# Two branches of cached attention for one token: one weight buffer split in two, K and V rings of four, the last V in pieces

## Chip, cores, metric

The kernel runs on one core of a Trainium2 chip. The metric is the device time of one execution in microseconds (us). Before the change it is 1589.96 us, the median of four runs (1573.62, 1588.67, 1591.26 and 1592.13). The run with a profile is the one of 1573.62 us; its trace spans 1571.9 us.

## What is computed

Two branches, A and B, have the same shape: one new token of width 512, 32 heads of width 128, and a cache of 8192 keys and values for each head, all in bf16. For each branch:

```python
q = (x @ wq) as 32 heads of 128          # x: 1 x 512, wq: 512 x 4096
scores = (q . k_cache) * 128 ** -0.5     # 8192 scores for each head
p = softmax(scores)
o = p . v_cache                          # 128 for each head
out = concat(o over heads) @ wo          # wo: 4096 x 512
# result: A's out and B's out side by side, 1 x 1024
```

The cache of one head is 2 MB of K and 2 MB of V, each read once. The kernel counts the heads of both branches through, n = 0 to 63; B begins with n = 32.

## The kernel before

K and V of a head lie in SBUF as 128 partitions by 64 keys by 128 values (`kb`, `vb`), in rings of three. Both wq and, later, both wo share one buffer `wb`. SyncE issues all loads; a load into a used place waits until its last reader is done.

```python
kb = SB("kb", [128, NK, JT, 128], BF)          # NK = 3, JT = 64
vb = SB("vb", [128, NV, JT, 128], BF)          # NV = 3
wb = SB("wb", [128, NBR, WSZ], BF)             # wq of both, then wo of both

# SyncE: x of both branches, then
for b in range(NBR):
    sp.dma_start(wb[:, b, ...], wqv[b]).then_inc(s_wq, 16)
def dma_k(n):
    if n >= NK:                                # the multiplies of head n-3 are done
        W(sp, s_tf, NE * (n - NK + 1)); W(sp, s_sttd, NDS * (n - NK + 1))
    sp.dma_start(kb[:, n % NK], ...)
def dma_v(n):
    if n >= NV:                                # P.V of head n-3 is done
        W(sp, s_pvd, n - NV + 1)
    sp.dma_start(vb[:, n % NV], ...)
def dma_wo(n):
    W(sp, s_qp, 1)                             # wq is no longer read
    if n >= 4: W(sp, s_pjd, n - 3)
    sp.dma_start(wb[:, b, h * DO:(h + 1) * DO], ...)
dma_k(0)
for n in range(N):
    if n + 1 < N: dma_k(n + 1)
    dma_v(n); dma_wo(n)
```

TensorE waits for both wq and projects q for all 64 heads, four matmuls each (L215), before anything else. Then all engines run one list of steps t, eight for each head. In slots 0, 2 and 4 of a head TensorE transposes eight blocks of K (L245), ScalarE copies them (`kt`, L349), and TensorE multiplies them by q (L259). In slots 1, 3, 5, 6 and 7 VectorE multiplies eight blocks each by a copy of q on all partitions (`qrep`) and sums along each row (L418). ScalarE copies TensorE's scores beside VectorE's (`ssb`, L356). The softmax needs the largest score and the sum over all partitions, which GpSimd makes:

```python
for n in range(N):                             # GpSimd
    W(pl, s_rmx, n + 1)
    pl.partition_all_reduce(gmx[n], mx[n], 128, ROP.max)            # L200
    pl.tensor_scalar(nb[n], gmx[n], -scale, None, AluOpType.mult)   # L202
    W(pl, s_expd, n + 1)
    pl.partition_all_reduce(gs[n], rs[n], 128, ROP.add)             # L204

# ScalarE, step 10 after the head's first
psb = exp(scale * ssb + nb), with the row sums in rs                # L332

# VectorE, in this order in its program
mx[n] = max of ssb (step 9)                                         # L387
rinv[n] = 1 / gs[n] (step 13, that is ahead of slot 5 of head n+1)  # L392
oT[n] = sum of P.V times rinv (step 20)                             # L398
```

P times V runs on TensorE in four blocks (L278) from step 12 on, ScalarE copies the result (`dsb`, L342), four small matmuls gather it (L298), and one matmul adds the head's part of the output projection (L311) into `misc`. After head 31 and head 63 VectorE casts `misc` to the output (`osb`, L405).

Of the kernel before, what the change touches and what calls it, by code (L numbers as in the profile page):

```python
# [7 lines left out]
def bass_concat_heads__mha_block_cached__gqa_block_cached__decode_kernel(  # L8
# [5 lines left out]
    NK, NV, LPV, NPE = 3, 3, 12, 3  # L14
# [16 lines left out]
    assert DH == 128 and D % 128 == 0 and SK % 2048 == 0  # L31
# [5 lines left out]
    assert DO <= 512 and N <= 64 and JT <= 64 and NG % 2 == 0  # L37
    NPS = NPE
    assert 1 <= NPS <= NG // 2

    def is_pe_slot(g):
        return g % 2 == 0 and g // 2 < NPS

    pe_slots = [g for g in range(NG) if is_pe_slot(g)]
    dv_slots = [g for g in range(NG) if not is_pe_slot(g)]
    NPT = 8 * len(pe_slots)
    colmap = {}
    for i, g in enumerate(pe_slots):
        for r in range(8):
            colmap[8 * g + r] = 8 * i + r  # L50
    for i, g in enumerate(dv_slots):
        for r in range(8):
            colmap[8 * g + r] = NPT + 8 * i + r
# [7 lines left out]
    WSZ = max(NCH * H * 128, H * DO)  # L61
# [3 lines left out]
    with ExitStack() as es:  # L65
# [12 lines left out]
        wb = SB("wb", [128, NBR, WSZ], BF)  # L78
# [26 lines left out]
        s_x = SEM("s_x"); s_wq = SEM("s_wq")  # L105
        s_wo0 = SEM("s_wo0"); s_wo1 = SEM("s_wo1"); s_wo2 = SEM("s_wo2"); s_wo3 = SEM("s_wo3")
        s_kl0 = SEM("s_kl0"); s_kl1 = SEM("s_kl1"); s_kl2 = SEM("s_kl2"); s_kl3 = SEM("s_kl3")
        s_vl0 = SEM("s_vl0"); s_vl1 = SEM("s_vl1"); s_vl2 = SEM("s_vl2"); s_vl3 = SEM("s_vl3")
        s_id0 = SEM("s_id0"); s_idr = SEM("s_idr"); s_slr = SEM("s_slr"); s_dz = SEM("s_dz")
        s_qp = SEM("s_qp"); s_qt = SEM("s_qt")  # L110
# [9 lines left out]
        assert NK <= 4 and NV <= 4  # L120
        s_kl = [s_kl0, s_kl1, s_kl2, s_kl3][:NK]
        s_vl = [s_vl0, s_vl1, s_vl2, s_vl3][:NV]
        s_wo = [s_wo0, s_wo1, s_wo2, s_wo3]
# [11 lines left out]
        LAST_PE_QK = max(pe_slots) + 2  # L135
        ST_RMAX = NG + 1
        ST_EXP = NG + 2
        ST_PV = max(LPV, NG + 4)
# [7 lines left out]
        NE = len(pe_slots)  # L146
        NDS = len(dv_slots)

        @block.sync
        def _(sp):  # L150
            with nc.allow_non_contiguous_dma(reason="tiny x transpose load"):
                for b in range(NBR):
                    sp.dma_start(xT[:, b, :], xv[b]).then_inc(s_x, 16)  # L153
            for b in range(NBR):
                sp.dma_start(
                    wb[:, b, 0:NCH * H * 128].rearrange("p (c m) -> p c m", c=NCH), wqv[b]
                ).then_inc(s_wq, 16)

            def dma_k(n):
                b, h = br_of(n)  # L160
                if n >= NK:
                    W(sp, s_tf, NE * (n - NK + 1))
                    W(sp, s_sttd, NDS * (n - NK + 1))
                sp.dma_start(kb[:, n % NK], kvw[b][:, h]).then_inc(s_kl[n % NK], 16)

            def dma_v(n):
                b, h = br_of(n)
                if n >= NV:
                    W(sp, s_pvd, n - NV + 1)
                sp.dma_start(vb[:, n % NV], vvw[b][:, h]).then_inc(s_vl[n % NV], 16)  # L170

            def dma_wo(n):
                b, h = br_of(n)
                W(sp, s_qp, 1)
                if n >= 4:
                    W(sp, s_pjd, n - 3)
                sp.dma_start(wb[:, b, h * DO:(h + 1) * DO], wov[b][:, h, :]).then_inc(s_wo[n % 4], 16)

            dma_k(0)
            for n in range(N):  # L180
                if n + 1 < N:
                    dma_k(n + 1)
                dma_v(n)
                dma_wo(n)
            for b in range(NBR):
                W(sp, s_accd, b + 1)
                sp.dma_start(out[0, 0:1, b * DO:(b + 1) * DO], osb[0:1, b, :]).then_inc(s_outd, 16)
            sp.wait_ge(s_outd, 16 * NBR)

        @block.gpsimd  # L190
        def _(pl):
            pl.memset(ones[:, :], 1.0).then_inc(s_id0, 1)
            pl.wait_ge(s_id0, 1)
            pl.affine_select(
                ident[:, :], ones[:, :], [[1, 128]], AluOpType.is_equal, 0.0,
                base=0, channel_multiplier=-1,
            ).then_inc(s_idr, 1)
            for n in range(N):
                W(pl, s_rmx, n + 1)
                pl.partition_all_reduce(gmx[:, n:n + 1], mx[:, n:n + 1], 128, ROP.max).then_inc(s_g1, 1)  # L200
                W(pl, s_g1, n + 1)
                pl.tensor_scalar(nb[:, n:n + 1], gmx[:, n:n + 1], -scale, None, AluOpType.mult).then_inc(s_nbr, 1)  # L202
                W(pl, s_expd, n + 1)
                pl.partition_all_reduce(gs[:, n:n + 1], rs[:, n:n + 1], 128, ROP.add).then_inc(s_gsr, 1)  # L204

        @block.tensor
        def _(pe):
            W(pe, s_x, 16 * NBR)
            W(pe, s_wq, 16 * NBR)
            last = None  # L210
            for n in range(N):
                b, h = br_of(n)
                wqb = wb[:, b, 0:NCH * H * 128].rearrange("p (c m) -> p c m", c=NCH)
                for c in range(NCH):
                    last = pe.matmul(  # L215
                        misc[:, n:n + 1], wqb[:, c, h * 128:(h + 1) * 128], xT[:, b, c:c + 1],
                        start=(c == 0), stop=(c == NCH - 1),
                    )
            last.then_inc(s_qp, 1)
            W(pe, s_idr, 1)  # L220

# [10 lines left out]
            for t in range(-16, TMAX):  # L232
                n, g = t // NG, t % NG
                if (t - ST_QREP) % NG == 0 and 0 <= (t - ST_QREP) // NG < N:
                    qrep_mm((t - ST_QREP) // NG)
                if 0 <= n < N and is_pe_slot(g):
                    e = g // 2
                    E = NE * n + e
# [10 lines left out]
                if 0 <= n2 < N and is_pe_slot(g2):  # L249
                    e = g2 // 2  # L250
                    E = NE * n2 + e
                    if e == 0:
                        if n2 == 0:
                            W(pe, s_qt, 1)
                        W(pe, s_qre, n2 + 1)
                    W(pe, s_ev, E + 1)
                    for i in range(8):
                        j = g2 * 8 + i
                        ins = pe.matmul(  # L259
                            sbk[n2 % 2][:, colmap[j]:colmap[j] + 1], kt[:, E % 2, i * 128:(i + 1) * 128],  # L260
# [4 lines left out]
                if tp >= 0 and tp // NG < N and (tp % NG) % 2 == 0 and (tp % NG) // 2 < JT // 16:  # L265
                    n3 = tp // NG
                    bt = (tp % NG) // 2
                    if bt == 0:
# [3 lines left out]
                        W(pe, s_vl[n3 % NV], 16 * (n3 // NV + 1))  # L272
                        if n3 >= 2:
                            W(pe, s_devd, n3 - 1)
                    for c in range(4):
                        i = 4 * bt + c
                        c0 = colmap[4 * i]
# [26 lines left out]
                if tj >= 0 and tj % NG == 0 and tj // NG < N:  # L304
# [3 lines left out]
                    W(pe, s_wo[n5 % 4], 16 * (n5 // 4 + 1))  # L308
                    if h == 0 and b > 0:
                        W(pe, s_accd, b)  # L310
                    pe.matmul(  # L311
                        misc[0:1, 0:DO], oT[:, n5:n5 + 1], wb[:, b, h * DO:(h + 1) * DO],
# [4 lines left out]
        def _(act):  # L317
            for t in range(-16, TMAX):
                n, g = t // NG, t % NG
                if (t - ST_QREP) % NG == 0 and 0 <= (t - ST_QREP) // NG < N:  # L320
                    m = (t - ST_QREP) // NG
                    W(act, s_qrm, m + 1)
                    if m >= 2:
                        W(act, s_sttd, NDS * (m - 1))
# [18 lines left out]
                if 0 <= n < N and is_pe_slot(g):  # L343
                    e = g // 2
                    E = NE * n + e
# [6 lines left out]
                tc = t - (LAST_PE_QK + 1)  # L352
                if tc >= 0 and tc % NG == 0 and tc // NG < N:
                    n8 = tc // NG
                    W(act, s_qkd, NE * (n8 + 1))
                    act.activation(ssb[:, n8 % 2, 0:NPT], sbk[n8 % 2][:, 0:NPT], AF.Copy).then_inc(s_scp, 1)  # L356

        @block.vector
        def _(dve):
# [8 lines left out]
            dve.tensor_copy(qT[:, :], misc[:, 0:N]).then_inc(s_qt, 1)  # L368

            def diag_op(m):  # L370
                W(dve, s_qt, 1)
# [6 lines left out]
            for t in range(-16, TMAX):  # L378
# [4 lines left out]
                if tr >= 0 and tr % NG == 0 and tr // NG < N:  # L383
                    n1 = tr // NG
                    W(dve, s_sttd, NDS * (n1 + 1))
# [20 lines left out]
                if 0 <= n < N and not is_pe_slot(g):  # L406
                    first = (g == dv_slots[0])
                    Sd = NDS * n + dv_slots.index(g)
                    if first:
                        W(dve, s_kl[n % NK], 16 * (n // NK + 1))  # L410
                        W(dve, s_qre, n + 1)
                        if n >= 2:
                            W(dve, s_expd, n - 1)
                    if Sd >= 2:
                        W(dve, s_sttd, Sd - 1)
                    for i in range(8):
                        j = g * 8 + i
                        ins = dve.scalar_tensor_tensor(  # L418
                            junk[:, (Sd % 2) * 8 + i, :], kb[:, n % NK, j, :], 1.0, qrep[:, n % 2, :],
                            AluOpType.mult, AluOpType.mult,  # L420
                            accum_out=ssb[:, n % 2, colmap[j]:colmap[j] + 1],
                        )
                    ins.then_inc(s_sttd, 1)
# [28 lines left out]
```

## Time and profile before

| what | busy us, or value |
|---|---|
| span of the trace | 1571.9 |
| VectorE (DVE) | 598.0 |
| TensorE (PE), and its weight loads (PEld) | 409.4, 244.7 |
| ScalarE (ACT) | 186.0 |
| GpSimd (POOL) | 67.4 |
| read from HBM | 285.21 MB, 181 GB/s over the span |
| granted TensorE clock | 0.578 of full speed on average |
| one multiply of VectorE (L418), x2560 | 287 ns |
| one PARTITION_ALL_REDUCE (L200, L204), x64 each | 379 and 402 ns as recorded |
| K and V, 2048 KB: issue to landing | 7.9 and 12.6 |

Busy times add up each engine's instructions. No engine is busy for more than 38% of the span, so these sums alone don't tell what sets the time. The profile has three further views that do: the list of waits (who stood idle, and which instruction released it), the chain that ended last (followed back from the last instruction, step by step), and the timeline of one engine. "issue" in them is time in which an engine waited for nothing that the profile shows. POOLq is GpSimd's instruction sequencer. GpSimd's recorded spans are rough.

### The profile page before, as it was taken

The page shows a single profiled execution, that of the slowest core. Times are in us where ns is not written, and L with a number is a line of the kernel's source. Part 1 is how long each engine was busy: PE and PEld are TensorE (multiplying, and loading weights), DVE is VectorE, ACT ScalarE, POOL GpSimd, SP SyncE. Part 2 cuts the span into 40 slices and gives each one's busy share as a digit, 9 for nine tenths or more (in the row PEclk, how much of TensorE's full clock was granted, in tenths as well). Part 3 has the DMA queues.
Part 4 walks back from the last instruction along what each step waited for, and adds up shares of the span by engine and source line. Part 5 has one row for each costly group of instructions (what it writes and reads, how often), then busy time and mean ns, then how long its engine had stood idle before and what let it go on. Part 6 is the DMA issues. An engine that isn't in the chain of part 4 may idle for free.

```text
span 1571.9 us, 17244 instructions
## 1 busy us (share of the span) xinstructions
PE 409.4 (26%) x4736; PEld 244.7 (16%) x4736; DVE 598.0 (38%) x5382; ACT 186.0 (12%) x513; POOL 67.4 (4%) x198
## 2 busy tenths in 40 slices
PE   2132221231322313313213223133132231321331
PEld 2111111111111101101111111011111110111110
DVE  1433433424434334244244343342442433424433
ACT  0011011010110101101101101011011010110110
POOL 0000000000000000000000000000000000000000
PEclk9855555555555555555555555555555555555555
DMA  9735435345354453453543544534535435355330
GB/s 381 303 136 221 181 150 221 149 182 212 124 217 171 161 221 141 191 215 134 202 191 141 221 166 165 221 139 193 202 136 215 175 157 221 127 204 207 133 159 0
DMA packets 29860, 286.33 MB, mean 182 GB/s; under 512 B 4162, under 2 KB 12356, under 8 KB 12356
## 3 DMA queue, kind: packets, MB, share of 16 engines
q1 hardware_dynamic: 29764, 285.23, 46.0%
q8 instruction: 38, 0.62, 0.2%
q14 instruction: 58, 0.48, 0.1%
HBM read 285.21 MB, written 0.00 MB: 181 GB/s over the span
## 4 chain that ended last, share of the span: by engine, by line
issue 69%; DVE 22%; POOL 4%; DMA 1%; ACT 1%; POOLq 1%; PE 1%; ACTq 0%; SPq 0%; DVEq 0%
DVE junk L418 21%; POOL gs L204 2%; POOL gmx L200 2%; DMA wb<-in_B_wq_dram 1%; POOL nb L202 1%; DVE mx L387 1%; ACT psb L332 1%; DVE rinv L392 1%; PE misc L215 0%; POOLq L65 0%; POOLq L202 0%; ACTq L130 0%; DVE osb L405 0%; SPq L153 0%; PE misc L311 0%
## 5 line engine op out<-in xcount | busy, mean ns | idle before, releaser
L418 DVE SCALAR_TENSOR_TENSOR junk<-kb,qrep 128x128 bf16<-128x128 bf16 x2560 | 557.7, 287 | 1.1 <-ACT qrep L325 0.8
L259 PE MATMUL sb<-qT,kt 128*128 128x1 bf16 x1536 | 73.7, 169 | 1091.5 <-ACT kt L349 1091.5
L398 DVE TENSOR_SCALAR oT<-sb,rinv 128x1 bf16<-128x1 f32 x64 | 14.1, 221 | 659.5 <-PE sb L298 659.4
L259 PEld LDWEIGHTS sb<-qT,kt 128*128 128x128 bf16 x1536 | 67.0, 109 | 1104.5 <-ACT kt L349 1104.2
L418 DVE DVE_READ_ACCUMULATOR junk<-kb,qrep 128x1 f32 x2560 | 210.9, 82 | 0.1
L245 PE MATMUL tb<-ident,kb 128*128 128x128 bf16 x1536 | 181.0, 292 | 0.0
L332 ACT ACTIVATE psb<-ssb,nb 128x64 bf16<-128x64 f32 x64 | 22.4, 350 | 1183.2 <-POOL nb L202 1183.2
L278 PE MATMUL db<-vb,psb 128*4 128x512 bf16 x1024 | 148.1, 568 | 15.8 <-ACT psb L332 15.8
L245 PEld LDWEIGHTS tb<-ident,kb 128*128 128x128 bf16 x1536 | 136.3, 132 | 101.7 <-issue 101.7
L349 ACT ACTIVATE kt<-tb 128x512 f32<-128x512 f32 x192 | 113.3, 590 | 108.1 <-PE tb L245 108.1
L392 DVE RECIPROCAL rinv<-gs 128x1 f32<-128x1 f32 x64 | 10.5, 164 | 276.0 <-POOL gs L204 276.0
L202 POOL TENSOR_SCALAR nb<-gmx 128x1 f32<-128x1 f32 x64 | 16.7, 261 | 712.3 <-issue 712.3
L204 POOL PARTITION_ALL_REDUCE gs<-rs x64 | 25.8, 402 | 389.3 <-issue 389.3
L311 PE MATMUL misc<-wb,oT 128*1 128x512 bf16 x64 | 40.3, 630 | 3.0 <-DVE oT L398 3.0
L200 POOL PARTITION_ALL_REDUCE gmx<-mx x64 | 24.3, 379 | 390.0 <-DVE mx L387 390.0
L342 ACT ACTIVATE dsb<-db 128x512 bf16<-128x512 f32 x64 | 37.5, 586 | 2.2 <-PE db L278 2.2
L278 PEld LDWEIGHTS db<-vb,psb 128*4 128x4 bf16 x1024 | 23.3, 81 | 32.5 <-ACT psb L332 16.7
L325 ACT ACTIVATE qrep<-sb 128x128 bf16<-128x128 f32 x64 | 17.8, 278 | 84.7 <-PE sb L228 84.7
L228 PE MATMUL sb<-diag,ones 128*128 128x128 bf16 x64 | 16.9, 264 | 22.7 <-issue 22.0
L298 PE MATMUL sb<-sel,dsb 128*128 128x1 bf16 x256 | 17.1, 170 | 0.7 <-ACT dsb L342 0.7
L298 PEld LDWEIGHTS sb<-sel,dsb 128*128 128x128 bf16 x256 | 11.8, 107 | 29.2 <-ACT dsb L342 28.8
L374 DVE TENSOR_SCALAR diag<-ident,qT 128x128 bf16<-128x128 bf16 x64 | 16.0, 251 | 0.0
(19 smaller groups left out, 69.1 us busy)
## 6 DMA issues: line engine op xcount, KB each, us to landing
kb<-in_A_k_cache_dram SPq DMA_DIRECT2D x32, 2048.0 KB, 7.9
vb<-in_A_v_cache_dram SPq DMA_DIRECT2D x32, 2048.0 KB, 12.6
kb<-in_B_k_cache_dram SPq DMA_DIRECT2D x32, 2048.0 KB, 7.7
vb<-in_B_v_cache_dram SPq DMA_DIRECT2D x32, 2048.0 KB, 12.5
wb<-in_A_wq_dram SPq DMA_DIRECT2D x1, 4096.0 KB, 13.1
wb<-in_B_wq_dram SPq DMA_DIRECT2D x1, 4096.0 KB, 22.5
wb<-in_A_wo_dram SPq DMA_DIRECT2D x32, 128.0 KB, 12.3
wb<-in_B_wo_dram SPq DMA_DIRECT2D x32, 128.0 KB, 12.3
```

Of the source, the lines that this page charges most:

```text
L200: pl.partition_all_reduce(gmx[:, n:n + 1], mx[:, n:n + 1], 128, ROP.max).then_inc(s_g1, 1)
L202: pl.tensor_scalar(nb[:, n:n + 1], gmx[:, n:n + 1], -scale, None, AluOpType.mult).then_inc(s_nbr, 1)
L204: pl.partition_all_reduce(gs[:, n:n + 1], rs[:, n:n + 1], 128, ROP.add).then_inc(s_gsr, 1)
L245: ins = pe.transpose(tb[E % 2][:, i * 128:(i + 1) * 128], kb[:, n % NK, j, :], ident[:, :])
L259: ins = pe.matmul(sbk[n2 % 2][:, colmap[j]:colmap[j] + 1], kt[:, E % 2, i * 128:(i + 1) * 128], qT[:, n2:n2 + 1], start=True, stop=True,)
L278: ins = pe.matmul(dbk[n3 % 2][32 * c:32 * c + 4, 0:512], psb[:, n3 % 2, c0:c0 + 4], vb[:, n3 % NV, 4 * i:4 * i + 4, :].rearrange("p a d -> ...
L298: ins = pe.matmul(sbk[(n4 + 1) % 2][:, OC:OC + 1], dsb[:, n4 % 2, m * 128:(m + 1) * 128], sel[:, m:m + 1], start=(m == 0), stop=(m == 3),)
L311: pe.matmul(misc[0:1, 0:DO], oT[:, n5:n5 + 1], wb[:, b, h * DO:(h + 1) * DO], start=(h == 0), stop=(h == H - 1),).then_inc(s_pjd, 1)
L332: act.activation(psb[:, n6 % 2, :], ssb[:, n6 % 2, :], AF.Exp, bias=nb[:, n6:n6 + 1], scale=scale, accum_out=rs[:, n6:n6 + 1],).then_inc(s ...
L342: act.activation(dsb[:, n7 % 2, :], dbk[n7 % 2][:, :], AF.Copy).then_inc(s_devd, 1)
L349: act.activation(kt[:, E % 2, :].bitcast(F32), tb[E % 2][:, :].bitcast(F32), AF.Copy,).then_inc(s_ev, 1)
L418: ins = dve.scalar_tensor_tensor(junk[:, (Sd % 2) * 8 + i, :], kb[:, n % NK, j, :], 1.0, qrep[:, n % 2, :], AluOpType.mult, AluOpType.mult ...
```

## The change

Three buffers are laid out anew, with no change to the arithmetic of a head.

- `wb` becomes `wqs`, which holds one branch's wq, and `wos`, a ring of eight for single heads' parts of wo. A's wq is loaded first, B's into the same place once A's has been read. TensorE projects A's q at the start, and B's in heads 8 to 15, four heads at a time. A PSUM bank of their own, `qpb`, takes the results. The aim is that the first head need not wait for B's weights.
- The rings of K and V have four places instead of three, so that loads may run further ahead.
- V of the last head is loaded in four pieces with a semaphore each, so that P times V may begin with the first of them.

The rest is renaming: the map "PDPDPDDD" states which engine takes which slot of a head.

```diff
-    NK, NV, LPV, NPE = 3, 3, 12, 3
+    NK, NV, NWO, QB0, VCH, MAP = 4, 4, 8, 8, 4, "PDPDPDDD"
...
-        wb = SB("wb", [128, NBR, WSZ], BF)
+        wqs = SB("wqs", [128, NCH, H * 128], BF)
+        wos = SB("wos", [128, NWO, DO], BF)
...
+        qpb = PS("qpb", [128, 512], F32)
...
-        LAST_PE_QK = max(pe_slots) + 2
-        ST_PV = max(LPV, NG + 4)
+        ST_PV = NG + 4
...
-            for b in range(NBR):
-                sp.dma_start(
-                    wb[:, b, 0:NCH * H * 128].rearrange("p (c m) -> p c m", c=NCH), wqv[b]
-                ).then_inc(s_wq, 16)
+            sp.dma_start(wqs[:, :, :], wqv[0]).then_inc(s_wq, 16)
...
-                sp.dma_start(vb[:, n % NV], vvw[b][:, h]).then_inc(s_vl[n % NV], 16)
+                if n == N - 1 and VCH > 1:
+                    jc = JT // VCH
+                    for c in range(VCH):
+                        sp.dma_start(
+                            vb[:, n % NV, c * jc:(c + 1) * jc, :], vvw[b][:, h, c * jc:(c + 1) * jc, :]
+                        ).then_inc(s_vlc[c], 16)
+                else:
+                    sp.dma_start(vb[:, n % NV], vvw[b][:, h]).then_inc(s_vl[n % NV], 16)
...
-                W(sp, s_qp, 1)
-                if n >= 4:
-                    W(sp, s_pjd, n - 3)
-                sp.dma_start(wb[:, b, h * DO:(h + 1) * DO], wov[b][:, h, :]).then_inc(s_wo[n % 4], 16)
+                if n >= NWO:
+                    W(sp, s_pjd, n - NWO + 1)
+                sp.dma_start(wos[:, n % NWO, :], wov[b][:, h, :]).then_inc(s_wo[n % NWO], 16)
+
+            def dma_wq_b():
+                W(sp, s_qp, 1)
+                sp.dma_start(wqs[:, :, :], wqv[1]).then_inc(s_wqb, 16)
...
+            # order of issue: k0, then k(n+1), v(n), wo(n); B's wq behind wo(2)
...
-            W(pe, s_wq, 16 * NBR)
+            W(pe, s_wq, 16)
             last = None
-            for n in range(N):
+            for n in range(H):
+                last = qproj(n)
             last.then_inc(s_qp, 1)
...
+            QPB = 4
+            qb_sched = {}
+            for i in range(0, H, QPB):
+                qb_sched[min(QB0 + i // QPB, H - 2) * NG + 1] = list(range(H + i, min(H + i + QPB, N)))
...
+                if t in qb_sched:
+                    if qb_left[0] == len(qb_sched):
+                        W(pe, s_wqb, 16)
+                    for nn in qb_sched[t]:
+                        ins = qproj(nn)
...
-            dve.tensor_copy(qT[:, :], misc[:, 0:N]).then_inc(s_qt, 1)
+            dve.tensor_copy(qT[:, 0:H], qpb[:, 0:H]).then_inc(s_qt, 1)
...
+                if m >= H and not qt2_done[0]:
+                    W(dve, s_qp2, 1)
+                    dve.tensor_copy(qT[:, H:N], qpb[:, H:N]).then_inc(s_qt2, 1)
```

(The comment on the order of issue stands for a loop that builds the list.)

## The prediction

> **What bounds the kernel now.** I read the list of waits first, to see whether any engine ever waits for a K or V load. Columns: engine and line that waited, what released it, total us, times, longest us.
>
> ```profile
> ACT psb L332 <- POOL nb L202: 1183.2, 64, 21.9
> POOL nb L202 <- issue: 712.3, 64, 12.6
> POOL gmx L200 <- DVE mx L387: 390.0, 64, 34.2
> POOL gs L204 <- issue: 389.3, 64, 8.4
> DVE rinv L392 <- POOL gs L204: 276.0, 64, 16.2
> PE misc L215 <- DMA wb<-in_B_wq_dram: 25.0, 1, 25.0
> DVE junk L418 <- ACT qrep L325: 0.8, 1, 0.8
> ```
>
> The only wait for a load is PE's for B's wq, once, 25.0 us. The multiplies (L418) never wait for K. The long waits lead to GpSimd, and GpSimd's own two are "issue": nothing recorded ended them.
>
> Next, the chain that ended last, for one head in the middle (start us, length us, what):
>
> ```profile
> 731.92 5.61 issue
> 737.53 0.41 POOL gs L204
> 737.95 0.02 issue
> 737.97 0.17 DVE rinv L392
> 738.13 3.86 DVE junk L418 x37
> ...
> 743.25 0.23 DVE mx L387
> 743.48 0.09 issue
> 743.57 0.38 POOL gmx L200
> 743.95 0.06 POOLq L202 x2
> 744.01 10.86 issue
> ```
>
> So each head is a closed loop: maximum over partitions (gmx), a gap of some 11 us, nb, exp, a gap of some 6 us, sum over partitions (gs), reciprocal, then the 24 multiplies of slots 5 to 7 (5.1 us), mx, and gmx of the next head. DVE's program order closes it: rinv of head n stands ahead of slots 5 to 7 of head n+1. "POOLq L202 x2" are two pool-configuration instructions ahead of the gap; the source view counts 128 on L202 and 128 on L204, two per switch.
>
> Third, the timeline of GpSimd alone, late, where K and V have run out (start, length, what, idle before it):
>
> ```profile
> 1502.28 0.26 POOL L202 TENSOR_SCALAR nb<-gmx 128x1 f32<-128x1 f32 x1 [10.62 <-issue]
> ...
> 1522.12 0.26 POOL L202 TENSOR_SCALAR nb<-gmx 128x1 f32<-128x1 f32 x1 [7.13 <-issue]
> ...
> 1542.24 0.26 POOL L202 TENSOR_SCALAR nb<-gmx 128x1 f32<-128x1 f32 x1 [7.65 <-issue]
> ...
> 1561.68 0.26 POOL L202 TENSOR_SCALAR nb<-gmx 128x1 f32<-128x1 f32 x1 [6.94 <-issue]
> ```
>
> The gap falls from 10.6 to about 7.2 us exactly when no load runs beside it. It isn't DVE: head 62's multiplies run in the gap at 1515 as before. So **the bound is GpSimd's switching between its kernels, and loads make one of the two switches longer.** The 61 gaps with loads average (712.3 - 21.72)/61 = 11.32 us, the last three 21.72/3 = 7.24; a load costs 4.08 us. Likewise the gap before gs is 8.38 us for head 0, where loads still run, and (389.3 - 8.38)/63 = 6.05 otherwise: 2.33 us. Windows of 4 us show why only one suffers: loads run at 311 to 422 GB/s from about 720 to 732 and at 12 GB/s or less until the next mx.
>
> [...]K lands in 7.9 us and V, issued behind it, in 12.6 (page, part 6)[...]; I treat the queue as first in, first out.
>
> **The change, part by part.**
>
> *Head schedule.* "PDPDPDDD" is the old assignment (PE in slots 0, 2, 4), NG+4 is the old 12, and the score copy keeps its slot 7. GpSimd's order is unchanged. Nothing in the loop of a head changes.
>
> *Start.* PE no longer waits for B's wq. The windows from 5 to 30 us average about 427 GB/s. At 0.425 MB per us a 4,096 KB weight takes 9.9 us, a K or V 4.9, a wo 0.3. A's wq lands at 1.83 + 13.1 = 14.9 us, B's at 2.37 + 22.5 = 24.9. Then 256 projections take until 33.74 with a 1.55 us break, and DVE's multiplies begin at 35.13. After: 128 projections at 6.09/223 = 27 ns are 3.5 us, 18.5 us, or 20 with the break; plus 35.13 - 33.74 = 1.4 us, so 19.9 to 21.5. K of head 0 now follows A's wq and lands at 14.9 + 4.9 = 19.8, just early enough. I take **20.6: a gain of 14.5 us**. It is on the path: the loop starts with it.
>
> *A longer burst of loads.* The first fill is now wq of A, K0, K1, V0, K2, V1, K3, V2 and wq of B, with small wo's: 14.9 + 7 x 4.9 + 3 x 0.3 + 9.9 = 60 us. K4 and V3, released at about 29 us, end near 70, K5 and V4, released near 55, near 80. Before, the burst ended at 60 (the windows show it), so only head 0's sum switch was hit. After, head 1's, at about 67 to 75 us, is hit too: **2.3 us lost, once**. Its maximum switch would have been hit anyway. From about 81 us the old rhythm holds.
>
> *Ring of four.* K of head n+4 instead of n+3 is issued when head n's multiplies end: the same moment in the head, the same 4 MB per head. V's wait shifts by one head likewise. So no steady gain. But loads run out one head earlier: the maximum switch of head 60 is undisturbed as well as those of 61 to 63. **4.1 us gained, at the end.**
>
> *Projection of B in heads 8 to 15.* 16 PE matmuls in each of 8 heads, 27 ns apart at full clock, perhaps double at the granted 0.55: about 1 us each. The score copy at 710.97 waits for DVE's mx at 719.63, so there are 8 us of slack. No cost. One extra cast, 0.22 us, falls while DVE waits for gs. No cost.
>
> *Wo ring of eight, V in four pieces.* The last V is issued at 1509.63 today, and PV of head 63 starts only after the exp at 1562: more than 50 us early. Pieces of a transfer that is hidden bring 0.
>
> *Sum.* gmx of head 0 starts 9.14 us after the multiplies (35.13 to 44.27): 29.7. Head 1: + 25.26 (as today) = 55.0. Head 2: + 24.08 + 2.33 = 81.4, where 24.08 is (1514.61 - 69.53)/60, today's mean period. Head 60: 58 more, 1478. Then three undisturbed periods at (1554.37 - 1514.61)/2 = 19.88: 1537.7. The tail from gmx of head 63 stays 1571.9 - 1554.37 = 17.5: a span of 1555.2, or 16.7 less. [...]I subtract it from the median: 1589.96 - 16.7 = **1573.3 us, 1% faster**.
>
> **Rivals.** (1) *Loads are the bound and a deeper ring frees them.* DMA's busy share is near half, and SP waits 1374 us for DVE. But SP waits because loads are ahead, and no engine waits for K or V. If true, the period itself would fall: one us of it is 64 us. (2) *Loads meet both switches in every head.* If the extra backlog never drained, 2.33 us x 62 heads = 144 us would be lost, near 1720. Against: a head's loads take some 10 us of a 24 us period, so the backlog must drain. The opposite, loads falling outside the maximum switch, would bring up to 4.08 x 60 = 245 us; the unchanged release moment speaks against it. (3) *B's projections lie on the path.* Even 2.5 us in eight heads is 20 us, which would cancel the gain; 8 us of slack speak against it.[...]
>
> **Range and chances.** The terms that I trust are 14.5 (+-2), -2.3 (+-2) and 4.1 (+-1): a gain of 13 to 20 us. The runs before spread by 18.5 us, mostly the gap before nb, which varies from 10.4 to 12.6 us with no visible cause; this is larger than my terms. So 1556 to 1587. Faster by over 2% needs less than 1558.2: possible if the new runs resemble the fastest old one, 0.12. Slower by over 2% needs rival 2 or 3 in a strong form: 0.02. Within 2%: 0.86.
>
> **What the profile after will show.** Multiplies start near 20 to 22 us, not 35; PE's first wait is for A's wq, some 15 us. The gap before gs is above 8 us for heads 0 and 1 and near 6 after. Gaps before nb near 11.3, the last four near 7.2. No K or V wait. DVE, ACT and POOL counts stay, but for one cast. The period from head 2 on stays 24.1 us: if it moves by half a microsecond, this prediction is wrong by 30 us, and the moments of the loads are where to look.

## The result, and the profile after

The changed kernel takes 1577.62 us (median of 11 runs, 1569.65 to 1586.53) against 1589.24 us for the kernel before (median of 16 runs, 1573.62 to 1600.79). The ratio is 0.9939, with a 95% interval of 0.991 to 0.9968: some 10 us faster, and well within 2%. The profiled run after took 1579.24 us and spans 1577.5 us. The profiled run before happened to be the fastest of its 16, so the two spans, 1571.9 and 1577.5, must not be compared as they stand; the parts can.

The list of waits after the change (what waited, what released it, total us, times, longest us):

```profile
ACT psb L375 <- POOL nb L213: 1201.5, 64, 23.2
POOL nb L213 <- issue: 728.2, 64, 15.4
POOL gs L217 <- issue: 394.2, 64, 9.6
POOL gmx L211 <- DVE mx L456: 375.0, 64, 19.2
...
PE qpb L229 <- DMA wqs<-in_A_wq_dram: 15.1, 1, 15.1
...
PE tb L279 <- DMA kb<-in_A_k_cache_dram: 2.4, 2, 2.0
```

The same waits head the list, with nearly the same sums: two "issue" gaps on GpSimd in every head. Two lines answer to the change. PE's wait for weights is 15.1 us and for A's only, where it was 25.0 us for both. K's loads are now waited for, 2.4 us in all, at the very start: the head start is so early that K0 and K1 have only just landed.

The chain that ended last, from its beginning (start us, length us, what):

```profile
1.84 13.09 DMA wqs<-in_A_wq_dram
14.94 0.14 issue
15.07 3.56 PE qpb L229 x128
...
19.98 1.79 DVE junk L440 x16
...
29.12 0.52 POOL gmx L211
29.64 0.07 POOLq L213 x2
29.71 11.53 issue
```

The multiplies start at 19.98 us instead of 35.13. The loop begins then, and it begins with the same gap behind the same two configuration instructions.

The end of GpSimd's timeline (start, length, what, idle before it):

```profile
1488.27 0.26 POOL L213 TENSOR_SCALAR nb<-gmx 128x1 f32<-128x1 f32 x1 [15.42 <-issue]
...
1508.09 0.26 POOL L213 TENSOR_SCALAR nb<-gmx 128x1 f32<-128x1 f32 x1 [6.74 <-issue]
...
1528.08 0.26 POOL L213 TENSOR_SCALAR nb<-gmx 128x1 f32<-128x1 f32 x1 [6.77 <-issue]
...
1547.66 0.26 POOL L213 TENSOR_SCALAR nb<-gmx 128x1 f32<-128x1 f32 x1 [6.91 <-issue]
...
1567.44 0.26 POOL L213 TENSOR_SCALAR nb<-gmx 128x1 f32<-128x1 f32 x1 [7.06 <-issue]
```

Four heads, 60 to 63, now have short gaps, where it was three. Head 60's is not quite free of loads: the last V still runs beside its first 2 us, at 370 GB/s. The last head with a full set of loads has a gap of 15.42 us, longer than any other ahead of nb in either trace, and directly ahead of the last V, which this version loads in four pieces. So the next question is whether the pieces cost what the ring gains.

### The profile page after: what moved, and what is told of

It is laid out like the page before. It is cut to its first block, busy times and chain, and to the rows that moved or that the text cites. A ratio compares the mean times of both kernels' runs of the same rounds, so it can differ in the third digit from the quotient of the medians.

```text
span 1577.5 us, 17156 instructions
## 1 busy us (share of the span) xinstructions
PE 417.5 (26%) x4736; PEld 249.6 (16%) x4736; DVE 598.2 (38%) x5383; ACT 186.0 (12%) x513; POOL 67.4 (4%) x198
## 4 chain that ended last, share of the span: by engine, by line
issue 70%; DVE 22%; POOL 4%; ACT 1%; DMA 1%; POOLq 1%; PE 0%; ACTq 0%; SPq 0%; DVEq 0%
DVE junk L440 21%; POOL gs L217 2%; POOL gmx L211 2%; POOL nb L213 1%; DVE mx L456 1%; ACT psb L375 1%; DMA wqs<-in_A_wq_dram 1%; DVE rinv L461 1%; POOLq L59 0%; POOLq L213 0%; PE qpb L229 0%; ACTq L123 0%; DVE osb L474 0%; SPq L144 0%; PE misc L354 0%
## 5 line engine op out<-in xcount | busy, mean ns | idle before, releaser
L279 PE MATMUL tb<-ident,kb 128*128 128x128 bf16 x1536 | 187.2, 299 | 2.4 <-DMA kb<-in_A_k_cache_dram 2.4
L279 PEld LDWEIGHTS tb<-ident,kb 128*128 128x128 bf16 x1536 | 140.5, 135 | 102.4 <-issue 99.7
L213 POOL TENSOR_SCALAR nb<-gmx 128x1 f32<-128x1 f32 x64 | 16.7, 261 | 728.2 <-issue 728.2
L217 POOL PARTITION_ALL_REDUCE gs<-rs x64 | 25.8, 402 | 394.2 <-issue 394.2
L354 PE MATMUL misc<-wos,oT 128*1 128x512 bf16 x64 | 40.3, 630 | 2.9 <-DVE oT L467 2.9
L211 POOL PARTITION_ALL_REDUCE gmx<-mx x64 | 24.3, 379 | 375.0 <-DVE mx L456 375.0
```

The lines of the kernel that those rows point to most:

```text
L279: ins = pe.transpose(tb[E % 2][:, i * 128:(i + 1) * 128], kb[:, n % NK, j, :], ident[:, :])
L354: pe.matmul(misc[0:1, 0:DO], oT[:, n5:n5 + 1], wos[:, n5 % NWO, :], start=(h == 0), stop=(h == H - 1),).then_inc(s_pjd, 1)
```

## The experiments

My theory: the loop is bound by GpSimd's switches from one of its two kinds of instruction to the other (the two "issue" gaps of a head), and the loads matter because they lengthen a switch. Its rivals: the supply of K and V is the bound; VectorE's multiplies, which run beside the gaps, lengthen them; or the partition reduction itself takes this long and only its record is short. The change itself has a second question: which part of it brings the gain?

### One part of the change at a time

**e1_start_only** keeps the split weight buffer alone:

```diff
-    NK, NV, NWO, QB0, VCH, MAP = 4, 4, 8, 8, 4, "PDPDPDDD"
+    NK, NV, NWO, QB0, VCH, MAP = 3, 3, 8, 8, 1, "PDPDPDDD"
```

> The changed kernel with rings of three for K and V and the last V in one piece: only the split weight buffer is left of the change. My theory (the gain is the early start; the ring only moves loads): gmx of head 0 near 29 us as with the whole change, but the first burst of loads ends near 60 us, so the gap before gs is long for head 0 only and gmx of head 2 starts near 81 us, not 83.5. At the end three short gaps before nb (about 7 us), not four. Gain against before 13 us less 2 to 4, about 10 us, ratio 0.994, the same as the whole change within 0.003. Rival (the deeper ring carries a good part of the gain): clearly slower than the whole change, ratio 0.997 or more.

Measured: 1572.98 us against 1581.32 us before on that chip, ratio 0.9935 (0.9912 to 0.9959). That is as much as the whole change brought in its own measurement. gmx of head 0 starts at 30.09 us, and three short gaps end the run (6.84, 7.03, 6.78). One detail was wrong: the gap before gs is long for head 1 too (9.05 us), and gmx of head 2 starts at 78.28. K4 and V3 still follow B's weights: at the prediction's 4.9 us each the first burst ends near 70 us, not at 60 (an estimate). With rings of four the loads run at 401 to 436 GB/s from 60 to 80 us in the profile after.

**e2_v_whole** keeps all but the pieces (VCH = 1 in the line above, NK and NV 4).

> The changed kernel with the last V in one piece. The profile after shows one odd gap before nb, 15.42 us for head 59, the last head with loads beside it. Theory 1 (the pieces have nothing to do with it, they are issued only 7 us after that gap ended, and it is chance): gap of head 59 between 10.5 and 13 us, time the same as the whole change within 0.3%. Theory 2 (the four pieces and their instructions cause it): gap of head 59 near 11.5 here and 15 in the whole change each time; 4 us faster.

Measured: 1566.12 us, ratio 0.9897 (0.9865 to 0.9929). The gap of head 59 is 11.83 us, the next four 7.17, 7.33, 7.01 and 6.78. It is 6.9 us faster than e1, which was measured beside it on the same chip (means differ by 5.2 us). So of the 15.2 us gained there (1581.32 - 1566.12), the start brings 8.3 and the rings of four the rest, as far as six and ten runs that spread by 10 and 13 us can tell: the rival to my theory was partly right. That e1 matched the whole change's own ratio does not speak against this, as that ratio comes from another set of runs. e2 also looks faster than the whole change had been, and the intervals overlap. So both were run side by side:

**e5_after_again** is the changed kernel unaltered.

> The changed kernel once more, beside the next run on the same chip, to see whether the odd gap of 15.42 us before nb of head 59 comes back. Chance: that gap is between 10.5 and 13 us now, ratio 0.990 to 0.994. Cause in the four pieces of the last V: the gap is again well above all others, 14 us or more, ratio near 0.994.

**e6_v_whole_again** is e2 once more, on the same chip.

> The changed kernel with the last V in one piece, on the same chip as the run before. Chance: same time as the changed kernel within 0.2%, ratio 0.990 to 0.994. Cause in the pieces: 4 to 7 us faster than the changed kernel.

Measured: 1565.68 us with the pieces, ratio 0.9896 (0.9862 to 0.993), and 1566.59 us without, ratio 0.99 (0.9862 to 0.9939). The gap of head 59 is 12.25 us with the pieces and 13.49 us without. So the pieces don't cause the long gap, and no gain or cost of theirs shows. That the gap is mere chance is not shown: head 59's is the longest of the whole run in the profile after, in e4 (12.00 us) and in e6. In both runs heads 60 to 63 have short gaps (6.6 to 7.1 us): from gmx of head 60 to that of head 63 it takes 58.5 us, where it took 63.1 before and 63.8 in e1 with rings of three. These 4 to 5 us are the part of the ring's gain that the traces show; with the spread of the runs they fit the 6.9 us between e1 and e2.

### What the loads do to the loop

**e3_no_loads** loads K and V for four heads only; the loads of the other 60 are left out. The cut shows K; V has the same line, the waits ask for the first four loads alone, and VCH is 1.

```diff
                 if n >= NK:
+                    return
```

> The changed kernel, but K and V are loaded for the first four heads only; all later heads read these again (the loads of 60 heads are left out, so it computes something else). Theory 1 (GpSimd's switches are lengthened by loads beside them): from head 3 on every gap before nb falls from 11.7 to about 7 us, the gap before gs stays near 6.0, the period falls from 24.4 to 19.9 us, and the time is about 83.5 + 61 x 19.8 + 17.5 + 2 = 1310 us. Rival A (data supply is the bound): far below that, as the multiplies would run back to back at 9.4 us a head, some 650 us. Rival B (the multiplies of VectorE lengthen the gap[...]): gap stays near 11.5 and the period at 24.4.

Measured: 1295.31 us. The waits of GpSimd:

```profile
POOL nb L217 <- issue: 449.7, 64, 9.7
POOL gs L221 <- issue: 389.7, 64, 8.1
```

The sum ahead of nb falls from 728.2 to 449.7 us; from head 3 on a gap is 6.96 us instead of 11.70. The sum ahead of gs stays (389.7 us against 394.2). The period is 19.68 us (24.46 in the changed kernel's profile). Without these loads (those of wo remain, 128 KB a head) the loop still takes four fifths of its time, so the supply of data is not the bound. VectorE's work is unchanged (GpSimd waits 375.4 us for mx, 375.0 in the profile after), so it isn't what makes a gap 11 us long. The loads are: they cost 4.7 us a head, through GpSimd.

**e4_loads_after_gs** releases each load later in the head, by one wait more on SyncE:

```diff
                     W(sp, s_sttd, ND * m)
+                    W(sp, s_gsr, m)
```

> The changed kernel, but K's load (and V's, which stands behind it) is released by the sum gs of the head, some 18 us later than the end of its multiplies. Nothing else changes. Theory 1: loads now begin some 2 us into the multiplies of slots 5 to 7 and run 10 us, so about half of them meets the switch before nb; its gap falls from 11.7 to about 9 us, the gap before gs stays near 6, the period is near 22 us, and the time falls by some 60 x 2.5 = 150 us to about 1430 (1400 to 1500). Rival A (data supply): later loads can only cost, time 1578 or more. Rival B[...]: no change of the gap, 1578.

Measured: 1518.78 us, ratio 0.9581 (0.9541 to 0.9621). Faster, but by much less than I expected: the gap before nb is 10.69 us, not 9. In the head at 712 us loads run beside the switch for about its first 6 us only (at 408 GB/s from 712.8 to 718.8, 5 GB/s from there to nb at 723.19), yet on average the switch loses 3.7 of the 4.7 us. The loss is not in proportion to the overlap. Nor is it the issuing of the loads that costs: SyncE issues this head's from 706.86 to 708.13, some 5 us before the switch begins. Two more runs ask what the loss follows.

**e9_k_only** halves each head's loads: V is loaded for four heads only, and the other 60 V loads are left out (VCH is 1 here too).

> The changed kernel, but V is loaded for the first four heads only and read again by all later ones (60 of the V loads are left out; it computes something else). Each head's loads now last 5 us instead of 10 and lie wholly in the first 7 us of the switch before nb. Theory a (the switch is lengthened in proportion to the time that loads run beside it): gap before nb near 9.2 us, halfway between 6.9 and 11.5, period near 22. Theory b (one part of the switch, its early one, is hit, and any load there costs nearly all of it; this is what the 10.7 us with the loads released by gs hint at): gap 10 to 11 us, period near 23.3.

**e10_loads_after_nb** is e4 with the wait on nb instead of gs.

> The changed kernel with the loads released by nb of the head, so that they run beside the switch before gs (6 us) and the start of the multiplies, and no longer beside the switch before nb. Theory 1: gap before nb falls from 11.6 to about 7 us, gap before gs rises from 6.05 to between 8 and 9.9 (what it was for heads 0 and 1, where loads ran beside it), the period falls from 24.3 to 22 to 23, time 1440 to 1500. If both switches suffer alike (4.5 us each) nothing is won: 1570.

Measured: e9 takes 1539.55 us, with a gap of 11.11 us, close to the full 11.6. Half the bytes cost nearly as much as all: theory b. Where in the switch they ran I can only estimate: in the profile after K is issued 0.28 us ahead of gmx (at 692.71) and lands 7.8 to 8.1 us after its issue, some 7 us into the switch. e10 takes 1530.64 us, ratio 0.9634 (0.9583 to 0.9685), at a period of 23.61 us; both lie outside what theory 1 expected (1440 to 1500 us, 22 to 23). Loads now run at 319 to 414 GB/s from 700 to 712 us, and at 4 GB/s or less from 712 to 720. The GpSimd timeline shows the two gaps changing places:

```profile
709.49 0.40 POOL L218 PARTITION_ALL_REDUCE gs<-rs  x1 [10.15 <-issue]
715.53 0.38 POOL L212 PARTITION_ALL_REDUCE gmx<-mx  x1 [5.64 <-DVE mx L457]
722.59 0.26 POOL L214 TENSOR_SCALAR nb<-gmx 128x1 f32<-128x1 f32 x1 [6.68 <-issue]
```

The gap before nb is down to 7.04 us on average, and that before gs up from 6.05 to 9.88: 4.5 us won, 3.8 given back. So either switch lost some 4 us where loads ran beside most of it.

Not just any load there counts. In the profile after, the last V runs at 370 GB/s beside the first 2 us of head 60's switch (1501.35 to 1503.35) and at 7 GB/s on average after that, and the gap is 6.74 us, as short as with no load. In e5, the same kernel, head 60's gap is 7.05 us; before, with head 61, it is 284 GB/s for 2 us, then 3 GB/s, and 7.13 us. So loads that stopped 2 us into a switch cost nothing, and loads that went on for 6 us (e4, 10.69 us) or by my estimate 7 us (e9, 11.11 us) cost nearly all. Whether the place matters or the amount (0.74 MB in those 2 us, 2 MB and more in e4 and e9) is not shown, and no run has loads in the late part of a switch alone. In the burst at the start (394 GB/s over the first 60 us of the profile after), however, the gap of head 0 lasts about 8 us in the experiments' profiles (7.90 in e1, 7.96 in e5) and 10.06 and 11.60 us in the profiles before and after, so "loads beside it" is not the whole condition. What a switch waits for stays open. The DMA queues don't tell: the two that carry instructions move 0.62 and 0.47 MB in the changed kernel and 0.62 and 0.44 MB in e8, below, which has no switch in its loop.

### The switch itself

**e7_before_nb_on_act** takes one instruction away from GpSimd in the kernel before. ScalarE makes nb ahead of its exp, so GpSimd's loop holds partition reductions only.

```diff
-                W(pl, s_g1, n + 1)
-                pl.tensor_scalar(nb[:, n:n + 1], gmx[:, n:n + 1], -scale, None, AluOpType.mult).then_inc(s_nbr, 1)
...
-                    W(act, s_nbr, n6 + 1)
+                    W(act, s_g1, n6 + 1)
+                    act.activation(nb[:, n6:n6 + 1], gmx[:, n6:n6 + 1], AF.Copy, scale=-scale).then_inc(s_nbr, 1)
+                    W(act, s_nbr, n6 + 1)
```

> The kernel before, but ScalarE makes nb (a copy of gmx with scale -scale) ahead of its exp, so GpSimd runs one kind of kernel only in the loop. Theory 1 (the bound is GpSimd's switch between kernels): both gaps go, the period falls from 24 to about 10 us, where the loads (4.3 MB at 0.425 MB per us, 10.1 us a head) or VectorE (598 us / 64 = 9.3 us a head) take over: 35 + 64 x 10.2 + 15 = about 700 us (660 to 800). Rival (the partition reduction itself takes the 6 to 11 us and its record is merely short): gaps stay ahead of the instruction that needs the result, time above 1400 us.

**e8_after_nb_on_act** does the same to the changed kernel.

> The changed kernel with nb made by ScalarE as in the run before. Theory 1: once the loop is bound by loads or VectorE at about 10 us a head, the changes count for more or less as follows: early start, 15 us less; the ring of four and the late load of B's weights don't change the bytes, so if loads are the bound B's weights cost their 10 us anyway and the gain over the run before is 5 to 15 us, about 690 us. If VectorE is the bound (9.4 us a head) the start's 15 us come through in full. Rival: above 1400 us.

Measured: 731.40 us, ratio 0.4621 (0.4604 to 0.4638), and 730.26 us, ratio 0.4614 (0.4597 to 0.4631), both against the unaltered kernel before. GpSimd's timeline in e8:

```profile
307.42 0.37 POOL L211 PARTITION_ALL_REDUCE gmx<-mx  x1 [8.51 <-DVE mx L456]
309.51 0.39 POOL L215 PARTITION_ALL_REDUCE gs<-rs  x1 [1.72 <-ACT psb L375]
318.74 0.37 POOL L211 PARTITION_ALL_REDUCE gmx<-mx  x1 [8.85 <-DVE mx L456]
```

No "issue" gap is left in the loop, where the kernel before has two in every head, each behind two pool-configuration instructions (128 on L202, 128 on L204). Each reduction starts when its input is there and its result is used at once (in e7 gmx of head 63 runs from 722.51 for 0.36 us, nb follows at 722.89). So the reductions are as short as recorded, and the 6 to 12 us were the price of a 0.26 us multiply of another kind between them. This settles the bound: 1,584 us of the kernel before become 731 by moving one instruction.

What bounds it then is the first rival, the supply of K and V. The waits for K in e8, and DMA's rate over 40 slices of the span:

```profile
PE tb L277 <- DMA kb<-in_A_k_cache_dram: 113.4, 32, 13.5
PE tb L277 <- DMA kb<-in_B_k_cache_dram: 106.6, 32, 4.4
```

```profile
GB/s 303 428 418 426 422 427 419 425 424 421 424 422 426 422 426 420 425 420 427 423 422 418 415 415 402 404 400 391 399 406 417 400 411 389 394 400 386 357 135 14
```

Every head now waits for its K, and the loads run without a pause. At this bound the change under study is worth 731.40 - 730.26 = 1.1 us, too little to tell from zero by the intervals; I had expected 5 to 15. The multiplies start 15 us earlier as before (at 20.97 us in e8, 36.34 in e7), but B's 4 MB of weights must be loaded in either order, and the loads before the change run at 412 to 429 GB/s from 5 to 50 us too (e7). With the transfers as the bound, the early start shortened next to nothing.

## Why the prediction was right, and where it was off

The prediction was 1573.3 us with a gain of 16.7; measured are 1577.62 us with 11.6 between the medians, and 18.4 (1584.12 - 1565.68) when the same kernel ran again. Both times lie in its range of 1556 to 1587. Of the gains, 18.4 lies in the stated 13 to 20 us and 11.6 below it. That the totals come this close is partly luck, as 16 runs of the kernel before spread by 27 us; the steps say more:

- **The bound** was read rightly: GpSimd's switches, from "issue" gaps behind pool-configuration instructions. e7 shows it by removing the switches. Undisturbed, a gap is 6.05 us before gs (before) and 6.96 us before nb (e3), and it is paid at every change between the two kinds of instruction, 128 times here. What GpSimd does in a gap, and by what means loads lengthen it, no run shows. And "exactly when no load runs beside it" was read too roughly: the last V runs beside the first 2 us of head 61's short gap.
- **Start:** multiplies at 19.98 us against 20.6 predicted, gmx of head 0 at 29.12 against 29.7. The break of 1.55 us in the projections did not recur. In e1 the start with its longer burst gains 8.3 us between medians (10.4 between means) where I had 14.5 - 2.3 = 12.2. The sign "no K or V wait" did not hold either: K0 and K1 are waited for, 2.4 us in all.
- **Longer burst:** head 1's gap before gs is long, as predicted (8.34 us here, 9.88 in e5), but the term was mis-sized. gmx of head 2 starts at 83.51 us in the profile after and at 79.31 in e5, against 81.4 predicted. From gmx of head 0 to gmx of head 2 it takes 49.4 us before, 54.4 after and 49.2 in e5: instead of a loss of 2.3 us a loss of 5.0 and a gain of 0.2. Head 0's gap before nb alone differs by 3.6 us between these two runs of one kernel. e1 shows besides that head 1's long gap doesn't need the ring.
- **No steady gain:** the period is 24.46 us in the profile after and 24.31 in e5. The profile before has 24.10, but it is the fastest of 16 runs; its median run is 15.6 us longer, which over 58 periods would make 24.37 (an estimate). So the loop is unchanged within what single traces can tell.
- **Ring:** four short gaps instead of three, some 4 to 5 us in the traces against 4.1 predicted, and 5.2 to 6.9 us between e1 and e2. In the profile after, the 15.42 us gap of head 59 hides it; e6 shows that a long gap there (13.49 us) doesn't need the pieces, and its cause stays open.
- **Projection of B, wo ring, pieces:** no cost and no gain shows. In the profile after the mean period of heads 8 to 15 is 24.39 us (24.46 over heads 3 to 60), a group of 16 matmuls for B's q takes some 0.6 us (0.58 at 248.44) where I had about 1, and e5 and e6 agree within 1 us.
- **Rival 2's other side** was wrong in size. I put the gain of moving the loads away from the maximum switch at up to 245 us. e10 moved them, and got back 3.7% of 1590 us, because the sum switch then loses 3.8 us. The loss was taken as a price for each load beside one switch; in e10 the other switch, with the loads beside it, paid it (9.88 us instead of 6.05).

Loads don't slow VectorE in the same way: in the profile after one of its 2560 multiplies takes 271 to 294 ns (median 286), though some run beside loads (383 GB/s from 1500.0 to 1503.3 us) and some beside none (from 713 to 717 us). A switch of GpSimd before nb takes 6.96 us without loads (e3) and 11.70 with them.

## What to carry to other kernels

An "issue" gap on GpSimd behind a pool-configuration instruction was here the cost of alternating between partition_all_reduce and tensor_scalar, and it bounded a kernel whose engines all look idle. Where a profile shows the same, move the odd small instruction to another engine first (1,584 us became 731 here). The early start and the deeper rings paid only their own few microseconds while a serial loop was the bound (11.6 and 18.4 us between medians), and next to nothing when the transfers were (1.1 us). A profile that is the fastest of its runs is no measure for another kernel's ordinary one: compare parts, and medians.

## What was unexpected of the hardware

Loads lengthened a GpSimd switch by about 4 us, and 2 MB a head did it nearly as much as 4: with 2 MB it took 11.1 us (e9), with 4 MB 11.6 us (e5), and with loads that ended after its first 6 us 10.7 us (e4), against 6.96 us with none (e3). Yet where loads stopped 2 us after its start it took 6.74 to 7.13 us. Loads moved from one switch to the other carried the loss with them (e10: 7.04 and 9.88 us instead of 11.6 and 6.05).
